# A gated MLP as seven products of halves: its roundings, copies and sums in another queue order, its late weight quarters made earlier, its v in four banks

## The chip, the cores and the metric

One NeuronCore of a Trainium2 chip runs the whole program in one launch. The time is microseconds (us) of device time; of several executions the median is taken. A profile of one more execution gives times from the span's start. The engines are TensorE (PE; PEld is its weight load), VectorE (DVE), ScalarE (ACT), GpSimd (POOL) and SyncE (SP), which issues the DMAs. Each engine works through its own queue in the order in which the code was written; an instruction that waits holds up all that stand behind it.

## The reference, cut to what matters

The input goes through three stages for 4 batches of 768 positions and 384 channels: a gated linear attention, a channel MLP with residual, and a gated MLP that mixes positions:

```python
ch = np.maximum(u @ w_ch1, 0.0) @ w_ch2          # second stage
x = u + ch                                       # (4, 768, 384), goes to x2d in HBM
h = np.maximum(x @ w_in, 0.0)                    # third stage, d_ff = 1024
u, v = h[..., :512], h[..., 512:]
v_n = (v - mean(v)) / np.sqrt(var(v) + 1e-06)    # over the 512 channels
v_s = np.einsum('ts,bsd->btd', w_spatial, v_n) + b_spatial[None, :, None]
out = (u * v_s) @ w_out
```

`w_spatial` is 768 x 768 and comes transposed.

## The kernel before

Matrices are held as two float32r parts, a rounded one (hi, `uh`, `vh`, names that end in h; the rounding is a copy on ScalarE) and the remainder (lo, `ul`, `vl`; `rest`, line 251, a subtraction of the two on VectorE or GpSimd). `mm3` (lines 286 to 288) multiplies two such pairs with three matmuls.

**Stages one and two.** For each batch the channel MLP runs over two blocks of 384 positions with 12 pieces of the inner width each: 24 groups per batch. A group is nine matmuls up (line 379), a ReLU with rounding on ScalarE (`h`, line 386), its remainder on VectorE (`hl`, line 367), and, two groups later, nine matmuls down (`mm3`). The up matmuls use two PSUM banks in turn, so a group can start when the `hl` of the group two before it has been read out of its bank. Between matmuls the code calls `pull()`, six times in a group and 144 times in a batch. With each pull other work is written into the queues, one step of a generator at a time, as many as `due()` allows. Under the first three batches' MLPs that is the attention of the next batch. Under the last batch's, "the last MLP" below, it is the preparation of stage three, `gating_steps`:

- the four quarters of `w_spatial` are loaded (`load_quads`, 576 KB each, in the buffers u0, u1, uh2 and ul2), rounded, combined and split into b11, b21, t3 and t4 (`quad_steps`);
- `w_in` and `w_out` are staged in 12 items through the same four buffers (`Stage`). An item is loaded, its float64 bits are turned to float32 by ScalarE (line 231), VectorE (lines 236 and 239) and an add on GpSimd (line 246); it is rounded by ScalarE (line 277), and VectorE makes the remainder (line 251). A step of the generator begins one item, rounds the one before it and makes the remainder of the one before that;
- the first half of the first batch's x is loaded and split, and three quarters are loaded again for the late parts t1, b22 and t2.

**Stage three**, class `Gating`. `v_n` is cut into 2 x 2 halves, and the product with `w_spatial` is made of seven products of halves (a11 b11, s3 t3, a12 b21, a22 t4, s2 t2, s1 t1, s4 b22) in place of eight. The steps for a batch are:

- `norm`: six tiles of v (`norm_steps`, nine matmuls of 512 columns each into a bank of PSUM), each copied out by ScalarE with ReLU (line 522), statistics on VectorE, then for three tiles together the square root on ScalarE (`z`, line 531), the normalisation (line 540), for the first half a difference (line 545), and for each tile a rounding (`vh`, line 503) and a remainder (`vl`);
- `sums` (lines 557 to 559): three sums per tile on VectorE, then the split of s1;
- `run`: four groups of u into the banks 4 to 7 (`first_half`), the seven products, copies of two of them out of PSUM (`kept`, lines 627 and 630), the split of s4 and s2 (`late_parts`), the gates (lines 589, 594, 596, a remainder on GpSimd), and the projection with `w_out` in two blocks (`project`; its banks are copied out by ScalarE at line 611).

The next batch's `norm` is called before the last projection of a batch and its `sums` after it; this passage from batch to batch is called a seam below. Before the change v goes to the banks 1 and 2 in turn (5 and 6 for the first batch), and the late parts t1, b22 and t2 are made inside the first batch's `norm`, a step between its tiles.

Of the kernel before, what the change touches and what calls it, by code (L numbers as in the profile page):

```python
# [36 lines left out]
F32 = mybir.dt.float32  # L37
# [23 lines left out]
F2 = DFF // 2  # L61
NF2 = F2 // 128
KE = E // 128
TB = 384
# [35 lines left out]
def gla_mixer_gating_kernel(ctx: ExitStack, tc: tile.TileContext, akq, v, vT, u, v3, w12, w_in, wsT, b_sp, w_out, out):  # L100
# [379 lines left out]
    class Gating:  # L480
# [3 lines left out]
        def __init__(self, g, wts, ap, psp, b, rooms=None, banks=(1, 2)):  # L484
# [4 lines left out]
        def norm(self, others=iter(())):  # L489

            a, b = self.norm_steps(0), self.norm_steps(1)
            for steps in (a, a, a, b, a, b, b, b):
                next(steps, None)
                next(others, None)
            drain(others)

        def split(self, names, c, x, engine=nc.gpsimd):

            tag = {"a11": f"{c}", "s4": f"{c}", "a12": f"{c + CB}", "s1": f"s{c}"}[names[0]]
            n = x.shape[1]  # L500
            hi = self.ap.tile([128, n], F32R, name="vh", tag=f"vh{tag}", bufs=1)
            lo = self.ap.tile([128, n], F32R, name="vl", tag=f"vl{tag}", bufs=1)
            nc.scalar.activation(out=hi, in_=x, func=AF.Copy)  # L503
            rest(lo, x, hi, engine)
            for i, name in enumerate(names):
                o = slice(i * F2 // 2, (i + 1) * F2 // 2)
                self.left[name][c] = hi[:, o], lo[:, o]

        def norm_steps(self, half):
# [3 lines left out]
            for j in range(CB):  # L513
                xh, xl = self.x2[half]
                ps = self.psp.tile([128, 512], F32, "ps_v", self.banks[(half * CB + j) % 2])
# [22 lines left out]
            for j in range(CB):  # L538
# [143 lines left out]
    def late_weights(wts, make, pool):  # L682

        tiles = [make(i, F32R) for i in range(5)]
# [5 lines left out]
        last, two = make(5, F32), pool.tile([128, 2 * TB], F32, name="kept", tag="u")  # L690
# [12 lines left out]
    def quad_steps(wts, raws):  # L703

        sp = wts["all"]
        w11, w12q, w22, w21 = raws
# [25 lines left out]
    def late_steps(wts, raws):  # L732
# [7 lines left out]
        combine(w12q, w12q, w11, nc.gpsimd)  # L740
        yield
        lo("b22", w22)
        yield
        hi("t1", w12q)
# [993 lines left out]
```

## Time and profile before

| | us |
|---|---|
| median of three runs (707.42 to 709.40) | 708.81 |
| the profiled execution, device time | 708.43 |
| its span, first to last instruction | 706.6 |
| TensorE busy | 671.7 (95%) |
| VectorE busy | 412.1 (58%) |
| ScalarE busy | 305.9 (43%) |
| GpSimd busy | 186.6 (26%) |
| mean granted TensorE clock, share of full | 0.982 |

The profiled execution's device time stands 1.8 us above its span. The two levels of TensorE's clock are 2.4 GHz (1.00 in the rows) and 1.2 GHz (0.50). The four seams lie at about 452, 522, 587 and 650 us, the last MLP between 355 and 439 us.

### The profile page before, as it was taken

How to read it: one execution, taken by the hardware profiler on the slowest of the kernel's cores; microseconds unless marked ns; L12 is line 12 of the kernel's file. 1: busy time of each engine (PE TensorE's matmuls, PEld its weight loads, DVE VectorE, ACT ScalarE, POOL GpSimd, SP SyncE). 2: the span in 40 equal slices, each digit the busy share in tenths (PEclk: the TensorE clock that was granted, in tenths of full speed). 3: DMA queues.
4: the chain of work that ended last, by engine and by line, in shares of the span. 5: the costliest groups of instructions: out<-in, count | busy, mean ns of one | idle time of the engine just before them, and what ended most of it. 6: DMA issues, size and time to landing. Idle time of an engine off the chain costs nothing.

```text
span 706.6 us, 14545 instructions
## 1 busy us (share of the span) xinstructions
PE 671.7 (95%) x6084; PEld 638.9 (90%) x6084; DVE 412.1 (58%) x762; ACT 305.9 (43%) x599; POOL 186.6 (26%) x169
## 2 busy tenths in 40 slices
PE   7989998999999999999998999799989998998995
PEld 6889987999999999999998999699879987997995
DVE  8989999665455344443336692774473455537441
ACT  3985366755555345454323343532243243233321
POOL 4520001151111301100300245406333440633041
PEclk9999999999999999999999999899989999999998
DMA  9699044444433005001033264202020202100001
GB/s 338 255 325 219 13 78 79 78 94 110 78 69 86 18 8 113 1 2 36 1 104 118 80 198 159 69 1 69 0 65 5 67 1 68 34 34 1 34 33 40
DMA packets 21644, 56.18 MB, mean 80 GB/s; under 512 B 2752, under 2 KB 12864, under 8 KB 20288
## 3 DMA queue, kind: packets, MB, share of 16 engines
q1 hardware_dynamic: 21568, 55.15, 28.5%
q8 instruction: 50, 0.82, 0.5%
q14 instruction: 26, 0.21, 0.1%
HBM read 44.52 MB, written 9.44 MB: 76 GB/s over the span
## 4 chain that ended last, share of the span: by engine, by line
PE 68%; DVE 21%; ACT 5%; issue 2%; DMA 2%; SPq 0%; ACTq 0%; DVEq 0%
PE banks L379 17%; PE banks L286 14%; PE banks L287 14%; PE banks L288 14%; DVE vt L540 2%; PE banks L1035 2%; DVE bw L906 2%; DVE fw L919 2%; DVE hl L367 1%; ACT vh L503 1%; DVE vt L545 1%; DVE narrow L239 1%; PE banks L993 1%; PE banks L1025 1%; PE banks L966 1%
## 5 line engine op out<-in xcount | busy, mean ns | idle before, releaser
L379 PE MATMUL banks<-partuh,w 128*128 128x384 f32 x564 | 131.7, 341 | 4.8 <-DVE hl L367 4.7
L379 PEld LDWEIGHTS banks<-partuh,w 128*128 128x128 f32 x564 | 99.9, 189 | 7.2 <-DVE hl L367 6.0
L367 DVE SCALAR_TENSOR_TENSOR hl<-banks,h 128x384 fp32r<-128x384 f32 x96 | 52.6, 548 | 83.2 <-ACT h L386 82.0
L286 PE MATMUL banks<-h,w 128*128 128x384 f32 x288 | 98.5, 342 | 0.2
L287 PE MATMUL banks<-h,w 128*128 128x384 f32 x288 | 96.7, 336 | 0.0
L288 PE MATMUL banks<-hl,w 128*128 128x384 f32 x288 | 96.5, 335 | 0.0
L386 ACT ACTIVATE h<-banks 128x384 fp32r<-128x384 f32 x94 | 45.5, 485 | 77.1 <-PE banks L379 76.9
L379 PE MATMUL banks<-partul,w 128*128 128x384 f32 x282 | 66.5, 344 | 0.0
L251 POOL TENSOR_TENSOR room<-room 128x384 fp32r<-128x384 f32 x32 | 32.5, 1017 | 112.7 <-ACT room L596 112.4
L895 POOL TENSOR_TENSOR akq<-akq,fw 128x768 f32<-128x768 f32 x14 | 23.6, 1685 | 142.6 <-DVE fw L919 125.3
L251 POOL TENSOR_TENSOR partul<-ub,partuh 128x384 fp32r<-128x384 f32 x43 | 42.6, 1016 | 65.4 <-ACT partuh L322 56.8
L286 PEld LDWEIGHTS banks<-h,w 128*128 128x128 f32 x288 | 54.2, 188 | 1.6 <-issue 0.8
L287 PEld LDWEIGHTS banks<-h,w 128*128 128x128 f32 x288 | 54.3, 188 | 0.0
L288 PEld LDWEIGHTS banks<-hl,w 128*128 128x128 f32 x288 | 54.2, 188 | 0.0
L379 PEld LDWEIGHTS banks<-partul,w 128*128 128x128 f32 x282 | 49.7, 190 | 0.8
L286 PE MATMUL banks<-partuh,winh 128*128 128x384 f32 x96 | 35.5, 370 | 14.4 <-ACT room L611 9.7
L503 ACT ACTIVATE vh<-vt 128x512 fp32r<-128x512 f32 (+1 forms) x48 | 26.4, 577 | 45.4 <-DVE vt L545 18.3
L596 ACT ACTIVATE room<-room 128x384 fp32r<-128x384 f32 x32 | 16.8, 525 | 67.3 <-DVE room L594 67.3
L251 DVE TENSOR_TENSOR vl<-vt,vh 128x512 fp32r<-128x512 f32 (+1 forms) x32 | 20.8, 672 | 29.5 <-ACT vh L503 28.0
L287 PE MATMUL banks<-partuh,winl 128*128 128x384 f32 x96 | 34.8, 362 | 0.0
L288 PE MATMUL banks<-partul,winh 128*128 128x384 f32 x96 | 34.6, 361 | 0.0
L895 POOL TENSOR_TENSOR akq<-akq,bw 128x768 f32<-128x768 f32 x11 | 18.6, 1691 | 60.3 <-DVE bw L906 49.8
(252 smaller groups left out, 1525.0 us busy)
## 6 DMA issues: line engine op xcount, KB each, us to landing
akq<-in_akq SPq DMA_DIRECT2D x24, 434.4 KB, 7.2
bits<-in_w SPq DMA_DIRECT2D x12, 768.0 KB, 11.6
x2d<-ub SPq DMA_DIRECT2D x8, 576.0 KB, 4.2
ub<-x2d SPq DMA_DIRECT2D x8, 576.0 KB, 4.3
out_y<-room SPq DMA_DIRECT2D x24, 192.0 KB, 2.0
v<-in_v SPq DMA_DIRECT2D x15, 288.0 KB, 8.1
words<-in_wsT SPq DMA_DIRECT2D x7, 576.0 KB, 5.0
words<-in_w_in SPq DMA_DIRECT2D x8, 384.0 KB, 3.6
```

Source lines behind the costliest of these rows:

```text
L251: engine.tensor_tensor(out=out, in0=x, in1=hi.bitcast(F32), op=ALU.subtract)
L286: nc.tensor.matmul(out=ps, lhsT=wh, rhs=xh, start=first, stop=False, skip_group_check=more)
L287: nc.tensor.matmul(out=ps, lhsT=wl, rhs=xh, start=False, stop=False, skip_group_check=more)
L288: nc.tensor.matmul(out=ps, lhsT=wh, rhs=xl, start=False, stop=last, skip_group_check=more)
L367: nc.vector.scalar_tensor_tensor(out=hl, in0=ps[:, 0:TB], scalar=0.0, in1=h.bitcast(F32), op0=ALU.max, op1=ALU.subtract)
L379: nc.tensor.matmul(out=ps[:, 0:TB], lhsT=wx[:, k * 128 : (k + 1) * 128], rhs=ux[:, k, :], start=i == 0, stop=i == len(parts) - 1)
L386: nc.scalar.activation(out=h, in_=ps[:, 0:TB], func=AF.Relu)
L503: nc.scalar.activation(out=hi, in_=x, func=AF.Copy)
L540: nc.vector.tensor_scalar(out=vt, in0=vt, scalar1=st[:, j, 0:1], scalar2=r[:, j : j + 1], op0=ALU.subtract, op1=ALU.mult)
L596: nc.scalar.activation(out=hi, in_=x, func=AF.Copy)
L895: engine.tensor_tensor(out=chunks(x)[:, c], in0=chunks(x)[:, c], in1=chunks(by)[:, c, 1:CW], op=ALU.mult)
L906: nc.vector.tensor_tensor_scan(out=bw[:, ::-1], data0=a[:, 1 : AW + 1][:, ::-1], data1=ends[:, ::-1], initial=0.0, op0=ALU.mult, op1=ALU.max)
```

## The change

- `split` becomes `splits`: for three tiles first all the roundings, then all the remainders, all of these on VectorE (before, four of the six remainders of a batch were GpSimd's).
- In `norm` the order is a, a, a, b, a, b, a, b, b: the splits of the first half come a step later, those of the second half are held back (`rest_of_norm`) until `sums`, which stands behind the projection. The split of s1 goes from `sums` to `late_parts`.
- v goes to the banks 1, 2, 4, 5, 1, 2 (first batch: 5, 6, 7, 5, 6, 7).
- `late_steps` runs in the last MLP's tail, from the 116th pull on, with its two combinations on VectorE instead of GpSimd; it no longer stands between the first batch's tiles of v.
- The generator of the last MLP takes a step at every third pull (before: 31 steps in 129 pulls, one in 4.16). The loads of the quarters stay at the 13th pull; their first use moves from the 21st to the 25th. The quarter that is needed second now is loaded second.

```diff
-        def __init__(self, g, wts, ap, psp, b, rooms=None, banks=(1, 2)):
+        def __init__(self, g, wts, ap, psp, b, rooms=None, banks=(1, 2, 4, 5, 1, 2)):
...
-        def norm(self, others=iter(())):
+        def norm(self):
             a, b = self.norm_steps(0), self.norm_steps(1)
-            for steps in (a, a, a, b, a, b, b, b):
+            for steps in (a, a, a, b, a, b, a, b, b):
                 next(steps, None)
-                next(others, None)
-            drain(others)
+            self.rest_of_norm = b
...
+        def splits(self, pieces):
+            made = []
+            for names, c, x in pieces:
...
+                nc.scalar.activation(out=hi, in_=x, func=AF.Copy)
+                made.append((lo, x, hi))
...
+            for lo, x, hi in made:
+                rest(lo, x, hi, nc.vector)
...
-                ps = self.psp.tile([128, 512], F32, "ps_v", self.banks[(half * CB + j) % 2])
+                ps = self.psp.tile([128, 512], F32, "ps_v", self.banks[half * CB + j])
...
-                    self.split(("a11", "s3"), j, vt)
-                else:
-                    self.split(("a12", "a22"), j, vt, nc.vector if j else nc.gpsimd)
+            yield
+            self.splits([(("a12", "a22") if half else ("a11", "s3"), j, self.vt[half * CB + j]) for j in range(CB)])
         def sums(self):
+            drain(self.rest_of_norm)
...
-            self.split(("s1",), c, a11, nc.vector)
         def late_parts(self):
-            for c in range(CB):
-                self.split(("s4", "s2"), c, self.vt[c + CB], nc.vector)
+            self.splits([(("s4", "s2"), c, self.vt[c + CB]) for c in range(CB)])
+            self.splits([(("s1",), c, self.vt[c][:, 0 : F2 // 2]) for c in range(CB)])
...
         def gating_steps():
             yield from check_alpha()
+            while pulls < 13:
+                yield
+            raws = load_quads(up.pool, RAW, (0, 3, 1, 2))
             yield
             yield
-            raws = load_quads(up.pool, RAW, range(4))
...
-            late_raws.extend(load_quads(up.pool, RAW[1:], range(3)))
+            raws = load_quads(up.pool, RAW[1:], range(3))
...
-            yield
+            while pulls < 116:
+                yield
+            late_weights(wts, late_tile)
+            yield from late_steps(wts, raws)
...
         def due():
+            if b == B - 1:
+                return -(-pulls // 3)
...
-        cur = Gating(g, wts, gpool, ps, 0, banks=(5, 6))
+        cur = Gating(g, wts, gpool, ps, 0, banks=(5, 6, 7, 5, 6, 7))
...
-        cur.norm(late_steps(wts, late_raws))
+        cur.norm()
```

TensorE's order stays the same but for one small matmul of the input check. Three places in the other queues follow; the line numbers of the change are its own.

ScalarE at a seam, before. `vt` is a v tile coming out of PSUM, `z` the square root, `vh` the rounding of a tile, `room<-banks` the copy of the projection out of its banks, `late<-banks` the copies of two products.

```order
L522 ACTIVATE vt<-banks 128x512 x4
L531 ACTIVATE z<-xe 128x3
L503 ACTIVATE vh<-vt 128x512 x3
L522 ACTIVATE vt<-banks 128x512 x2
L531 ACTIVATE z<-xe 128x3
L503 ACTIVATE vh<-vt 128x512 x3
L611 ACTIVATE room<-banks 128x384 x3
L503 ACTIVATE vh<-vt 128x256 x3
L627 ACTIVATE late<-banks 128x384 x2
L630 ACTIVATE late<-banks 128x384 x2
```

The same place of the change:

```order
L525 ACTIVATE vt<-banks 128x512 x4
L534 ACTIVATE z<-xe 128x3
L525 ACTIVATE vt<-banks 128x512
L504 ACTIVATE vh<-vt 128x512 x3
L525 ACTIVATE vt<-banks 128x512
L534 ACTIVATE z<-xe 128x3
L614 ACTIVATE room<-banks 128x384 x3
L504 ACTIVATE vh<-vt 128x512 x3
L630 ACTIVATE late<-banks 128x384 x2
L633 ACTIVATE late<-banks 128x384 x2
L504 ACTIVATE vh<-vt 128x512 x3
L504 ACTIVATE vh<-vt 128x256 x3
```

The three copies of the projection now stand ahead of the second half's roundings, and the roundings of s1 (128x256) behind the copies of the products.

VectorE in the last MLP, before, while `w_in` is staged. L236 and L239 belong to the item that is begun, L251 is the remainder of the one two before it, `hl` the remainder that a group of the MLP needs.

```order
L367 SCALAR_TENSOR_TENSOR hl<-banks,h 128x384
L251 TENSOR_TENSOR winl<-words,winh 128x384
L236 TENSOR_SCALAR words<-words 128x384
L239 SCALAR_TENSOR_TENSOR words<-words 128x384
L367 SCALAR_TENSOR_TENSOR hl<-banks,h 128x384
L251 TENSOR_TENSOR winl<-words,winh 128x384
L236 TENSOR_SCALAR words<-words 128x384
L239 SCALAR_TENSOR_TENSOR words<-words 128x384
L251 TENSOR_TENSOR winl<-words,winh 128x384
```

The same place of the change:

```order
L367 SCALAR_TENSOR_TENSOR hl<-banks,h 128x384
L251 TENSOR_TENSOR winl<-words,winh 128x384
L236 TENSOR_SCALAR words<-words 128x384
L239 SCALAR_TENSOR_TENSOR words<-words 128x384
L251 TENSOR_TENSOR winl<-words,winh 128x384
L236 TENSOR_SCALAR words<-words 128x384
L239 SCALAR_TENSOR_TENSOR words<-words 128x384
L367 SCALAR_TENSOR_TENSOR hl<-banks,h 128x384
```

Two items now stand between one group's `hl` and the next, where one or two stood before.

VectorE at the end of the last MLP, before. `ub` are the sums that end the MLP, `s` and `mv` the statistics of v tiles, `late` the remainders of the late parts.

```order
L367 SCALAR_TENSOR_TENSOR hl<-banks,h 128x384 x4
L439 TENSOR_TENSOR ub<-banks,ub 128x384 x3
L524 BN_STATS s_5018<-vt 128x6
L525 BN_AGGR mv<-s_5018 128x2
L524 BN_STATS s_5034<-vt 128x6
L525 BN_AGGR mv<-s_5034 128x2
L251 TENSOR_TENSOR late<-words,late 128x1152
L524 BN_STATS s_5049<-vt 128x6
```

The same place of the change:

```order
L367 SCALAR_TENSOR_TENSOR hl<-banks,h 128x384 x3
L706 TENSOR_TENSOR words<-words 128x1152
L367 SCALAR_TENSOR_TENSOR hl<-banks,h 128x384
L251 TENSOR_TENSOR late<-words,late 128x1152
L706 TENSOR_TENSOR words<-words 128x1152
L367 SCALAR_TENSOR_TENSOR hl<-banks,h 128x384
L251 TENSOR_TENSOR late<-words,late 128x1152
L251 TENSOR_TENSOR late<-words,late 128x384 x3
L367 SCALAR_TENSOR_TENSOR hl<-banks,h 128x384 x3
L439 TENSOR_TENSOR ub<-banks,ub 128x384 x3
L527 BN_STATS s_5028<-vt 128x6
```

The late parts, combinations (L706) and remainders, went from among the v tiles into the MLP's last groups.

## Rows read from the trace of the kernel before

**Rows 1.** The page's groups: xcount | busy, mean ns | idle before, releaser.

```profile
L367 DVE SCALAR_TENSOR_TENSOR hl<-banks,h 128x384 fp32r<-128x384 f32 x96 | 52.6, 548 | 83.2 <-ACT h L386 82.0
```

**Rows 2.** Timeline of TensorE, four waits: start, us, what, [idle before <-releaser].

```profile
376.94 0.92 PE L379 MATMUL banks<-partuh,w 128*128 128x384 f32 x2 [2.61 <-DVE hl L367]
...
457.32 0.69 PE L286 MATMUL banks<-partuh,winh 128*128 128x384 f32 x1 [4.70 <-ACT vt L522]
...
471.81 0.44 PE L286 MATMUL banks<-wspb21h,vh 128*128 128x384 f32 x1 [0.86 <-ACT late L627]
...
525.14 0.69 PE L286 MATMUL banks<-partuh,winh 128*128 128x384 f32 x1 [3.25 <-ACT room L611]
```

**Rows 3.** Stretches after waits: length, busy by engine, PEclk, DMA share, GB/s.

```profile
376.90:380.50 3.60, 3.56 (x11) 3.56 (x12) 3.57 (x4) 0.92 (x1) 0.00 (x0) 0.53 0.00 0
457.30:462.40 5.10, 5.08 (x16) 5.08 (x17) 4.59 (x15) 0.73 (x3) 0.00 (x0) 0.50 0.00 0
525.10:530.70 5.60, 5.56 (x17) 5.56 (x18) 4.90 (x13) 2.01 (x5) 0.00 (x0) 0.50 0.66 211
590.30:596.00 5.70, 5.65 (x32) 5.65 (x33) 4.91 (x13) 2.50 (x6) 0.00 (x0) 1.00 0.68 211
653.40:656.90 3.50, 3.48 (x11) 3.48 (x12) 3.14 (x9) 1.56 (x4) 0.00 (x0) 0.52 0.47 169
```

**Rows 4.** Timeline of ScalarE at the seam after 518 us.

```profile
519.25 0.20 ACT L531 ACTIVATE z<-xe 128x3 f32<-128x3 f32 x1 [1.49 <-DVE xe L530]
...
521.07 1.15 ACT L503 ACTIVATE vh<-vt 128x512 fp32r<-128x512 f32 x2 [1.62 <-DVE vt L540]
...
524.62 1.23 ACT L611 ACTIVATE room<-banks 128x384 f32<-128x384 f32 x3
```

**Rows 5.** Timeline of VectorE at the same seam.

```profile
511.34 0.55 DVE L540 TENSOR_SCALAR vt<-vt,mv,r 128x512 f32<-128x512 f32 x1
...
513.18 1.52 DVE L540 TENSOR_SCALAR vt<-vt,mv,r 128x512 f32<-128x512 f32 x1
...
524.74 0.69 DVE L251 TENSOR_TENSOR vl<-vt,vh 128x512 fp32r<-128x512 f32 x1 [0.69 <-ACT vh L503]
...
526.72 0.42 DVE L251 TENSOR_TENSOR vl<-vt,vh 128x256 fp32r<-128x256 f32 x1
```

**Rows 6.** Timeline of GpSimd at the same seam.

```profile
513.09 2.75 POOL L251 TENSOR_TENSOR vl<-vt,vh 128x512 fp32r<-128x512 f32 x2 [7.03 <-ACT vh L503]
```

**Rows 7.** The chain that ended last, in the last MLP: start, us, what.

```profile
388.13 1.56 PE banks L379 x9
...
416.61 1.86 PE banks L379 x9
```

**Rows 8.** Timeline of ScalarE, last MLP, first roundings of the quarters.

```profile
374.75 1.16 ACT L707 ACTIVATE wspb21h<-words 128x1152 fp32r<-128x1152 f32 x1 [4.63 <-DMA words<-in_wsT]
```

**Rows 9.** Tile words, 360 to 392 us: ns min/median/max, first and last start.

```profile
L701 DVE TENSOR_TENSOR words<-words x4: 1347/1350/1359, 376.8 to 384.7; 128x1152 f32<-128x1152 f32 x4
```

**Rows 10.** The page's DMA issues: KB each, median us from issue to landing.

```profile
words<-in_w_in SPq DMA_DIRECT2D x8, 384.0 KB, 3.6
```

**Rows 11.** Timeline of GpSimd, adds of the weight staging, last MLP.

```profile
402.98 1.02 POOL L246 TENSOR_TENSOR words<-words 128x384 uint32<-128x384 uint32 x1 [1.08 <-ACT words L231]
...
406.82 1.12 POOL L246 TENSOR_TENSOR words<-words 128x384 uint32<-128x384 uint32 x1 [2.82 <-DVE words L239]
...
411.62 1.03 POOL L246 TENSOR_TENSOR words<-words 128x384 uint32<-128x384 uint32 x1 [1.51 <-ACT h L386]
...
414.16 1.12 POOL L246 TENSOR_TENSOR words<-words 128x384 uint32<-128x384 uint32 x1 [1.51 <-ACT h L386]
...
416.41 1.02 POOL L246 TENSOR_TENSOR words<-words 128x384 uint32<-128x384 uint32 x1 [1.13 <-ACT words L231]
```

**Rows 12.** Timeline of TensorE and GpSimd, second batch's first projection.

```profile
549.61 0.34 PE L286 MATMUL banks<-wouth,room 128*128 128x384 f32 x1
...
549.81 2.07 POOL L251 TENSOR_TENSOR room<-room 128x384 fp32r<-128x384 f32 x2 [0.84 <-ACT room L596]
```

More of the change, by code (lines that the diff above doesn't have):

```diff
@@ L680, in thirds, with late_weights @@
         return [t[:, i * TB : (i + 1) * TB] for i in range(CB)]
-    def late_weights(wts, make, pool):
-        tiles = [make(i, F32R) for i in range(5)]
+    def late_weights(wts, make):
+        tiles = [make(i) for i in range(5)]
         for i, x in enumerate(LATE[0:2]):
@@ L689, in late_weights, with kept_rooms @@
         wts["sp"][LATE[2]] = [free[0:CB], free[CB : 2 * CB]]
-        last, two = make(5, F32), pool.tile([128, 2 * TB], F32, name="kept", tag="u")
+    def kept_rooms(last, pool):
+        two = pool.tile([128, 2 * TB], F32, name="kept", tag="u")
         return [*thirds(last), last[:, QUAD : QUAD + TB], two[:, 0:TB], two[:, TB : 2 * TB]]
@@ L705, in quad_steps @@
         sp = wts["all"]
-        w11, w12q, w22, w21 = raws
+        w11, w21, w12q, w22 = raws
         hi = lambda n, x: nc.scalar.activation(out=sp[n][0], in_=x, func=AF.Copy)
@@ L739, in late_steps @@
         hi("b22", w22)
-        combine(w12q, w12q, w11, nc.gpsimd)
+        combine(w12q, w12q, w11, nc.vector)
         yield
+        hi("t1", w12q)
         lo("b22", w22)
         yield
-        hi("t1", w12q)
-        combine(w11, w22, w12q, nc.gpsimd)
+        combine(w11, w22, w12q, nc.vector)
         yield
-        yield
-        lo("t1", w12q)
         for x, h, _ in t2:
             nc.scalar.activation(out=h, in_=x, func=AF.Copy)
-        yield
+        lo("t1", w12q)
         yield
@@ L1497, in gating_steps, with late_tile @@
             x2_first.append(load_x2(0, 1, up))
-            yield
+            while pulls < 116:
+                yield
+            late_weights(wts, late_tile)
+            yield from late_steps(wts, raws)
         pulls, done = 0, 0
-        x2_first, late_raws = [], []
+        x2_first = []
+        def late_tile(i, ty=F32R):
+            return wp0.tile([128, QUAD + TB], ty, name="late", tag=f"f{i}")
         def pull():
@@ L1541, in gla_mixer_gating_kernel @@
                 gating = Stage(gp, gating_items(wts), [(up.pool, x, KE * TB) for x in RAW])
-                steps, n_steps = gating_steps(), len(gating.items) + 19
+                steps = gating_steps()
             pulls, done = 0, 0
@@ L1560, in gla_mixer_gating_kernel @@
         spatial_bias(g, cp)
-        kept = late_weights(wts, lambda i, ty: wp0.tile([128, QUAD + TB], ty, name="late", tag=f"f{i}"), cp)
-        cur = Gating(g, wts, gpool, ps, 0, banks=(5, 6))
+        cur = Gating(g, wts, gpool, ps, 0, banks=(5, 6, 7, 5, 6, 7))
         cur.x2 = [x2_first[0], split_x2(x2_first[1], up, 1)]
-        cur.norm(late_steps(wts, late_raws))
+        cur.norm()
         cur.sums()
-        cur.rooms = GatingRooms(up.pool, kept)
+        cur.rooms = GatingRooms(up.pool, kept_rooms(late_tile(5, F32), cp))
         for b in range(B):
@@ L1658, in gla_mixer_gating_kernel @@
                 wts2 = gating_weights(gw2)
-                kept2 = late_weights(wts2, lambda i, ty: gw2.tile([128, QUAD + TB], ty, name=f"late{i}"), cp2)
-                drain(quad_steps(wts2, load_quads(up2.pool, RAW, range(4))))
+                late_tile2 = lambda i, ty=F32R: gw2.tile([128, QUAD + TB], ty, name=f"late{i}")
+                late_weights(wts2, late_tile2)
+                kept2 = kept_rooms(late_tile2(5, F32), cp2)
+                drain(quad_steps(wts2, load_quads(up2.pool, RAW, (0, 3, 1, 2))))
                 drain(late_steps(wts2, load_quads(up2.pool, RAW[1:], range(3))))
```

17 lines of the change are left out of this document (7 added, 10 removed).

## The prediction

> **What bounds the kernel now.** I read the page's busy times first (the table above), then its groups of instructions, then TensorE's timeline for its idle stretches, then the queue of the engine that ended each. TensorE is busy 95% of the span, so the time can fall only where it waits or runs at half clock. From the last MLP on, the timeline has six waits of 0.8 us or more; four stand in [rows 2], and the third and fourth seam repeat the 3.25 us of its last row. Three facts are to be seen in them.
>
> The wait before 376.94 us, 2.61 us, is released by VectorE's `hl` (0.55 us each, and itself mostly waiting for `h` [rows 1]), but the root is in ScalarE's queue: there the rounding of the second quarter waited 4.63 us for a DMA and ran only at 374.75 [rows 8], with two groups' `h` behind it. That quarter was the last of four to be loaded.
>
> The waits of 4.70 and 3.25 us end with a copy out of PSUM on ScalarE. TensorE needs a bank whose contents have long been complete, and the copy stands behind three roundings. At 521.07 two roundings run, the third after VectorE has normalised its tile, and only at 524.62 the three copies of the projection [rows 4]. The wait of 0.86 us is the same with the copies of two products.
>
> After four of the five waits of over 2.5 us the granted clock was at the lower level. TensorE then ran busy for 3.56, 5.08, 5.56 and 3.48 us at 0.50 to 0.53; after the third seam it stayed at 1.00 [rows 3].
>
> **What the change takes away at the seams.** TensorE's order is kept, so I ask for each wait whether its releaser comes early enough. In the new ScalarE queue the three copies of the projection need only `z` ahead of them. With `z` as late as now, 519.25 + 0.20 [rows 4], a first copy of 0.5 us ends at about 520, and TensorE needs its bank at 525.14 - 3.25 = 521.9 [rows 2]: 1.9 us to spare. Does `z` come later? On VectorE three remainders of 0.69 us [rows 5] now stand ahead of the last statistics, 2.1 us. In return GpSimd no longer makes two remainders there (2.75 us for two [rows 6]), during which a normalisation took 1.52 instead of 0.55 us [rows 5] and the difference behind it grew alike: about 1.9 us back. So `z` moves by about 0.2, and all three 3.25 us go.
>
> At the first seam the last v tile's copy still stands behind three roundings, but its bank is needed only by the fourth group of u, not the second, and the late parts are gone from between. I estimate 1.6 us to spare there and take 4.70 as gone. The 0.86 us goes because the roundings of s1 now stand behind the copies of the products. The moved remainders of the second half run under the four groups of u and two products, ten of TensorE's microseconds; if that cover failed, the products would wait as the copies do now.
>
> Waits: 4.70 + 0.86 + 3 x 3.25 = 15.3 us. With them go the half-clock stretches at three seams: 5.08/2 + 5.56/2 + 3.48 x 0.48 = 7.0 us [rows 3]. Together -22.3 us.
>
> **What the change does in the last MLP.** First the quarters. The second one used is now the second loaded, and one group's `h` stands between the two roundings, so the 2.61 us wait and 3.56 x 0.47 = 1.7 us of half clock behind it [rows 3] go: 4.3 us. VectorE then has six operations of 1.35 us [rows 9] between the landing of the last quarter (374.75, [rows 8]) and the end of t4's remainder, with three `hl` of 0.55 between, and one rounding of 1.16 that it waits for. That gives 374.75 + 8.1 + 1.7 + 1.2 = 385.8, less half a microsecond that overlaps: 385.3. Each `hl` falls 0.3 to 0.8 us before its group would start, so nothing waits yet.
>
> Then the items. The second item's buffer is free at 385.3; its load takes 3.6 us [rows 10], and from there to the add I take 1.3 us, which is GpSimd's idle time between two adds, where VectorE makes the same steps (1.1 to 1.5 [rows 11]). Its add on GpSimd starts at about 390.2. How fast can items follow? The adds of now come every 2.54 us where a group's `hl` stands between (411.62 to 414.16) and 2.25 us where none does (414.16 to 416.41); with the three closing sums of a block between it was 3.84 (402.98 to 406.82) [rows 11]. The cycle is VectorE's: the remainder is held up while GpSimd's add runs, then the next item's two steps follow, then the next add. Nothing in the change shortens it. With one `hl` to two items it is 2.4 us, and the block's three sums add 1.4. But the generator now asks for an item every third pull, half a group, and a group is 3.12 us long (416.61 - 388.13 is 9 groups and 0.4 us [rows 7]): an item every 1.56 us. Now it asks at every 4.16th pull, 2.16 us, and the queues fall behind only slowly.
>
> So from the second item on VectorE sets TensorE's pace, since a group's `hl` stands behind two items and the group after next cannot start without it. The eleventh item's add starts at 390.2 + 9 x 2.4 + 1.4 = 413.2. The `hl` of the 15th group stands just before it, so the 17th group starts at 413.6. The `hl` of the 16th stands behind another item and a remainder: about 417.0, where the 18th starts; the 19th starts at 420.1. Now it starts at 416.61 [rows 7]: +3.5 us, the 4.3 us saved before included. Before the 17th group TensorE waits 3.1 us, as long as at the seams, two of which in three were followed by half clock. I take 3.4 us of it, 1.7 us lost, 1.5 after the 18th group's wait has covered a little. Last MLP: +5.0 us.
>
> The late parts cost nothing in the tail. They are four operations of 1.35 us [rows 9] and three of a third of the size, 7 us of VectorE, in four groups of 3.12 us where `hl` takes 0.55 each. If that cover were gone, the first tiles of v would start up to 2 us later. Their loads are issued as the last items free their buffers, some 7 us ahead of the first use. TensorE's order is otherwise unchanged, and no part before the last MLP moves.
>
> **The sum.** Span 706.6 - 22.3 + 5.0 = 689.3 us. The profiled execution stood 1.8 above its span, at 708.43, which is 0.4 below the median of the runs shown: **691.1 us**.
>
> **A rule of the skill beside the row.** A normalisation that met GpSimd's remainders took 1.52 instead of 0.55 us [rows 5, 6], and the adds' interval is short only where a remainder ran ahead of the add [rows 11]. The Trainium skill, "SBUF — State Buffer", section "Who interferes with whom", says that a VectorE instruction with two SBUF inputs and a GpSimd instruction that reads SBUF exclude each other, the second waiting for the whole of the first. The rows agree as far as they go. By the rule taken strictly no remainder would run beside an add and every item would take the longer interval, 2.54 us: the sum would be 9 x 0.14 = 1.3 higher, 692.4. By the rows it is 691.1.
>
> **Rivals.**
>
> - *The pace does not hold TensorE.* If the slack between `h` and `hl` swallows the items, the last MLP loses its 4.3 us and the 0.4 at the 19th group and gains nothing: 706.6 - 22.3 - 4.7 + 1.8 = 681.4. For it: now the adds fall behind their pulls too, at 0.3 us an item, and TensorE lost just 0.4. Against it: eleven items fall behind by 0.8 each, 9 us, and two banks give about 3. 0.14.
> - *Every remainder is held up*, 2.54 us an item as worked out above, or an item takes still longer while TensorE's clock is low: 692.4 to 695. Nothing forbids it, since the two kinds of interval mix by chance. 0.16.
> - *The later gates starve the projection.* Three remainders of 0.42 us [rows 5] now stand ahead of the first gates, 1.3 us. GpSimd's remainder for the third quarter of the projection ends at 549.81 + 1.03 = 550.8 (half of two); the projection begins at 549.61 [rows 12], its third quarter 18 matmuls of 0.175 us later, 552.8. 1.9 us of slack become 0.7. From 1.9 us of delay on TensorE would wait; at 1.5 us in each of four batches: 697. 0.10.
> - *The change does not do what it says*: `z` comes 2 us later than now, so the copies are still late and a wait of 1 to 3 us with its half clock stays at the seams: 698 to 706. Against it the balance of 2.1 and 1.9 above. 0.04.
> - *Slower than before.* The pace eats the seams' 22.3 us. For that the last MLP would have to lose 17.3 us more than forecast, and an item take 17.3/9 = 1.9 more than 2.4: 4.3 us. The longest interval now is 3.84, with three extra sums in it [rows 11]. 0.02.
>
> **Numbers.** The forecast as worked out, 688 to 692.4, has 0.54. Its unknowns are the item's cycle (2.25 to 2.54 us: -1.4 to +1.3), the half clock (0 or 1.5) and the start of the items (1 us either way). Its own range with the second rival is 687 to 695. The range 684 to 698 takes in both, the third rival and a part of the first: about 0.82. A measurement of this kernel can tell 0.3% (2.1 us) from no change. Faster 0.96, same 0.02, slower 0.02.
>
> **What would show it.** Right: no TensorE idle over 0.5 us at the four seams and a clock of 1.00 there; ScalarE's copies of the projection within 1 us of the end of its matmuls; no wait before the 7th group of the last MLP; then adds on GpSimd every 2.2 to 2.6 us, with TensorE waiting 1 to 3 us for `hl` before each of the 13th to 18th group, and the 24th group starting about 4 to 5 us later than now. Wrong: items at 1.6 us without such waits (681), or waits at the first projection or at the first gates of the batches (697), or a seam whose copies come behind `z` at 521 or later.

## The result, and the profile after

The changed kernel takes **689.19 us** (median of 4 runs, 688.84 to 690.38); the kernel before took 708.12 beside it (706.89 to 709.4). The ratio is 0.9736, 95% interval 0.9713 to 0.9759. The forecast was 691.1. The profiled execution took 689.03 us, its span is 687.1 (706.6 before). Its page begins:

```profile
PE 664.9 (97%) x6084; PEld 633.3 (92%) x6084; DVE 411.3 (60%) x780; ACT 305.8 (45%) x599; POOL 159.6 (23%) x151
```

The span falls by 19.5 us. The first tile of v starts at 441.92 us (438.59 before), so the part before it got 3.3 us longer and the rest, from there to the end, went from 268.0 to 245.2 us: 22.8 shorter. The sum of TensorE's waits from 355 us on (engine and line that waits, releaser: us, times, longest) holds nothing of a seam any more:

```profile
PE banks L286 <- DVE ub L439: 3.5, 1, 3.5
PE banks L379 <- DVE hl L367: 2.5, 2, 1.4
```

All three are in the last MLP. Of before [rows 2], the 2.61, 4.70, 0.86 and the three 3.25 are gone. Stretches of the changed kernel, with the columns of [rows 3] (length, busy time of PE, PEld, DVE, ACT and POOL, PEclk, DMA share, GB/s):

```profile
407.40:411.20 3.80, 3.72 (x13) 3.75 (x14) 3.73 (x8) 1.59 (x4) 1.45 (x2) 0.55 0.57 190
454.00:471.00 17.00, 17.00 (x98) 16.96 (x97) 16.06 (x41) 8.58 (x18) 0.00 (x0) 1.00 0.00 1
514.00:531.00 17.00, 17.00 (x99) 17.00 (x98) 10.09 (x23) 6.61 (x14) 0.00 (x0) 1.00 0.22 69
```

At these two seams TensorE is busy without a break at full clock, and so it is at the other two (573 to 590 and 633 to 650 us). Up to its last matmul half clock is left once, after the longest wait of the last MLP.

The seam on ScalarE, which answers to [rows 4]:

```profile
512.98 0.20 ACT L534 ACTIVATE z<-xe 128x3 f32<-128x3 f32 x1 [2.50 <-DVE xe L533]
513.09 1.41 ACT L614 ACTIVATE room<-banks 128x384 f32<-128x384 f32 x3
514.80 1.67 ACT L504 ACTIVATE vh<-vt 128x512 fp32r<-128x512 f32 x3 [0.30 <-DVE vt L543]
```

The copies of the projection (L614, L611 before) run right behind `z`, the three roundings behind them. The same seam on VectorE, which answers to [rows 5]:

```profile
508.32 0.54 DVE L543 TENSOR_SCALAR vt<-vt,mv,r 128x512 f32<-128x512 f32 x1
508.89 0.42 DVE L548 TENSOR_TENSOR vt<-vt 128x256 f32<-128x256 f32 x1
509.23 0.69 DVE L527 BATCH_NORM_STATS2 s<-vt 128x6 f32<-128x512 f32 x1
...
510.05 1.86 DVE L251 TENSOR_TENSOR vl<-vt,vh 128x512 fp32r<-128x512 f32 x3
511.83 0.69 DVE L527 BATCH_NORM_STATS2 s<-vt 128x6 f32<-128x512 f32 x1
...
512.77 0.17 DVE L533 TENSOR_SCALAR xe<-mv 128x3 f32<-128x3 f32 x1
```

No row here has idle time ahead of it. The third normalisation takes 0.54 us (1.52 before), the fifth tile's statistics stand ahead of the three remainders, and VectorE goes straight on to `xe`.

The adds of the items on GpSimd, which answer to [rows 11]:

```profile
390.01 1.22 POOL L246 TENSOR_TENSOR words<-words 128x384 uint32<-128x384 uint32 x1 [2.13 <-ACT h L386]
...
406.72 1.01 POOL L246 TENSOR_TENSOR words<-words 128x384 uint32<-128x384 uint32 x1 [1.14 <-ACT words L231]
409.82 1.11 POOL L246 TENSOR_TENSOR words<-words 128x384 uint32<-128x384 uint32 x1 [2.09 <-DVE words L239]
412.07 1.02 POOL L246 TENSOR_TENSOR words<-words 128x384 uint32<-128x384 uint32 x1 [1.14 <-ACT words L231]
```

Eight adds lie from 390.01 to 406.72, 2.39 us each; with the closing sums of the first block between two of them the interval is 3.10. And VectorE in the same stretch, from one `hl` past the next:

```profile
396.77 0.55 DVE L367 SCALAR_TENSOR_TENSOR hl<-banks,h 128x384 fp32r<-128x384 f32 x1
397.24 1.37 DVE L251 TENSOR_TENSOR winl<-words,winh 128x384 fp32r<-128x384 f32 x1
398.53 0.35 DVE L236 TENSOR_SCALAR words<-words 128x384 uint32<-128x384 uint32 x1
...
399.39 0.55 DVE L251 TENSOR_TENSOR winl<-words,winh 128x384 fp32r<-128x384 f32 x1
399.86 1.19 DVE L236 TENSOR_SCALAR words<-words 128x384 uint32<-128x384 uint32 x1
...
401.56 0.55 DVE L367 SCALAR_TENSOR_TENSOR hl<-banks,h 128x384 fp32r<-128x384 f32 x1
...
406.31 0.55 DVE L367 SCALAR_TENSOR_TENSOR hl<-banks,h 128x384 fp32r<-128x384 f32 x1
406.78 1.48 DVE L439 TENSOR_TENSOR ub<-banks,ub 128x384 f32<-128x384 f32 x3
```

Two whole items (L251, L236 and, left out here, L239 of each) stand between two `hl`, and the engine never idles: 4.79 us for what TensorE does in 3.12. In each item one instruction that runs beside GpSimd's add is long (1.37 instead of 0.55, 1.19 instead of 0.35). TensorE pays for it here (its timeline, as in [rows 2]):

```profile
397.38 0.79 PE L379 MATMUL banks<-partuh,w 128*128 128x384 f32 x3 [1.09 <-DVE hl L367]
...
402.16 0.79 PE L379 MATMUL banks<-partuh,w 128*128 128x384 f32 x3 [1.39 <-DVE hl L367]
...
407.48 0.41 PE L286 MATMUL banks<-h,w 128*128 128x384 f32 x1 [3.48 <-DVE ub L439]
```

The last is the first matmul down of the second block. It needs an accumulator bank which the closing sums (L439) free, and these stand behind two items and an `hl`. From 407.48 to 450 us TensorE has no wait of 0.4 us or more.

### The profile page after: what moved, and what is told of

Its sections match the earlier page's. It is cut to its first block, busy times and chain, and to the rows that moved or that the text cites. A ratio compares the mean times of both kernels' runs of the same rounds, so it can differ in the third digit from the quotient of the medians.

```text
span 687.1 us, 14557 instructions
## 1 busy us (share of the span) xinstructions
PE 664.9 (97%) x6084; PEld 633.3 (92%) x6084; DVE 411.3 (60%) x780; ACT 305.8 (45%) x599; POOL 159.6 (23%) x151
## 4 chain that ended last, share of the span: by engine, by line
PE 76%; DVE 15%; ACT 3%; DMA 3%; issue 2%; SPq 0%; DVEq 0%; ACTq 0%
PE banks L286 17%; PE banks L288 17%; PE banks L287 17%; PE banks L379 16%; PE banks L1038 2%; DVE bw L909 2%; DVE fw L922 2%; PE banks L996 1%; DVE hl L367 1%; PE banks L1028 1%; DVE narrow L239 1%; PE banks L969 1%; DVE narrow L246 1%; PE banks L953 1%; DVE w L251 1%
## 5 line engine op out<-in xcount | busy, mean ns | idle before, releaser
L251 POOL TENSOR_TENSOR room<-room 128x384 fp32r<-128x384 f32 x32 | 32.5, 1016 | 168.4 <-ACT room L599 168.2
L251 POOL TENSOR_TENSOR partul<-ub,partuh 128x384 fp32r<-128x384 f32 x43 | 42.6, 1017 | 76.5 <-ACT partuh L322 56.8
L251 DVE TENSOR_TENSOR vl<-vt,vh 128x512 fp32r<-128x512 f32 (+1 forms) x48 | 26.6, 616 | 20.4 <-ACT vh L504 20.4
L288 PE MATMUL banks<-partul,winh 128*128 128x384 f32 x96 | 32.1, 334 | 0.0
L288 PE MATMUL banks<-woutl,room 128*128 128x384 f32 x96 | 32.1, 334 | 0.0
L286 PE MATMUL banks<-wouth,room 128*128 128x384 f32 x96 | 32.1, 334 | 0.0
L287 PE MATMUL banks<-wouth,room 128*128 128x384 f32 x96 | 32.1, 334 | 0.0
```

Source lines behind the costliest of these rows:

```text
L251: engine.tensor_tensor(out=out, in0=x, in1=hi.bitcast(F32), op=ALU.subtract)
L286: nc.tensor.matmul(out=ps, lhsT=wh, rhs=xh, start=first, stop=False, skip_group_check=more)
L287: nc.tensor.matmul(out=ps, lhsT=wl, rhs=xh, start=False, stop=False, skip_group_check=more)
L288: nc.tensor.matmul(out=ps, lhsT=wh, rhs=xl, start=False, stop=last, skip_group_check=more)
```

## The experiments

Times are medians beside runs of the kernel before on the same chip, in brackets the ratio's 95% interval. The changed kernel stands at 0.9736 (0.9713 to 0.9759).

**1. The kernel before, remainders behind all three normalisations.** GpSimd keeps its remainders, the banks and the place of the copies stay.

```diff
                     nc.vector.tensor_tensor(out=y, in0=x, in1=y, op=ALU.subtract)
+            for j in range(CB):
+                vt = self.vt[half * CB + j]
+                if half == 0:
                     self.split(("a11", "s3"), j, vt)
```

> The kernel before with one edit: in each half the three tiles are normalised first, then rounded, then their remainders made (before: tile by tile). Engines, banks, late parts, pace, and the place of the projection's copies behind the roundings all stay. The prediction's theory (the copies are late because they stand behind the roundings): the wait of 3.25 us stays at the three later seams to within 1 us; 706 to 709 us. The rival (the roundings were late only because VectorE made a remainder, held up by GpSimd's, ahead of the third normalisation): by the trace of before, z comes about 1.9 us earlier and the third rounding another 1.5 us, the waits fall below 0.5 us and the half clock goes with them: 708.1 - 9.8 - 4.4 = 694 us, within 2.

699.17 us, 0.9863 (0.9831 to 0.9895): between the two. TensorE's waits:

```profile
PE banks L286 <- ACT vt L522: 4.7, 1, 4.7
PE banks L286 <- ACT room L614: 3.8, 3, 1.3
```

Each 3.25 became 1.28, without half clock behind it. ScalarE shows why it is not zero:

```profile
519.62 0.20 ACT L531 ACTIVATE z<-xe 128x3 f32<-128x3 f32 x1 [1.49 <-DVE xe L530]
521.44 1.67 ACT L503 ACTIVATE vh<-vt 128x512 fp32r<-128x512 f32 x3 [1.62 <-DVE vt L540]
523.01 1.24 ACT L614 ACTIVATE room<-banks 128x384 f32<-128x384 f32 x3
```

The third rounding no longer waits for a normalisation that stands behind a remainder, but the copies still stand behind all three.

**2. The kernel before, copies of the projection first.** Only the second half's split moves behind the copies.

```diff
                 next(others, None)
             drain(others)
+            self.rest_of_norm = b
...
-                    self.split(("a12", "a22"), j, vt, nc.vector if j else nc.gpsimd)
+                    continue
+            if half:
+                yield
+                for j in range(CB):
+                    self.split(("a12", "a22"), j, self.vt[CB + j], nc.vector if j else nc.gpsimd)

         def sums(self):
+            drain(self.rest_of_norm)
```

> The kernel before with one thing altered: the roundings and remainders of the second half of v stand behind the copies of the projection. Engines, banks, and the order in the first half stay as before. Theory A, of the prediction: the three waits of 3.25 us were the place of the copies in ScalarE's queue, behind three roundings. All three go, with two stretches of half clock; the first seam keeps its 4.70, and the time is 694 to 697. Theory B, from the run in which the remainders stood behind the normalisations: of each 3.25 us some 2 is the remainder ahead of the third normalisation and 1.28 the place of the copies. In this kernel both go as well, because the remainder now stands behind both; but z itself is as late as before, so at most 0.3 us of wait is left and the time is 694 to 698. What would speak against both: waits of over 1 us at these three seams, and over 700 us.

694.48 us, 0.9812 (0.9789 to 0.9834), as both theories had it. The waits that are left:

```profile
PE banks L286 <- ACT vt L523: 4.7, 1, 4.7
PE banks L379 <- DVE hl L367: 3.3, 2, 3.0
```

All three waits of 3.25 us are gone, though `z` comes no earlier than before and GpSimd keeps its remainders. The 0.86 went too.

**3. The changed kernel, copies behind the roundings again.**

```diff
-            for steps in (a, a, a, b, a, b, a, b, b):
+            for steps in (a, a, a, b, a, b, a, b, b, b):
```

> The changed kernel with the split of the second half put back ahead of the projection's copies in ScalarE's queue; remainders on VectorE, four banks, pace and late parts stay. The prediction's theory: the copies are late again, 3.25 us and its half clock at three seams: 700 to 703 us. The rival: in the changed kernel's trace the third rounding ends at 516.47 and TensorE needs the bank at about 516.9, so the copies come 0 to 0.5 us late: 689 to 691 us.

690.67 us, 0.9747 (0.9715 to 0.9778), not told apart from the changed kernel, and no seam waits, as the rival had it.

```profile
512.74 0.20 ACT L534 ACTIVATE z<-xe 128x3 f32<-128x3 f32 x1 [2.51 <-DVE xe L533]
514.56 1.68 ACT L504 ACTIVATE vh<-vt 128x512 fp32r<-128x512 f32 x3 [1.62 <-DVE vt L543]
516.14 1.23 ACT L614 ACTIVATE room<-banks 128x384 f32<-128x384 f32 x3
```

**4. The changed kernel, four of the six remainders on GpSimd as before.**

```diff
+                engine = nc.gpsimd if names[0] == "a11" or (names[0] == "a12" and c == 0) else nc.vector
-                rest(lo, x, hi, nc.vector)
+                rest(lo, x, hi, engine)
```

> The changed kernel with four of six remainders of a batch back on GpSimd (all of the first half, the first of the second). Both theories of order: no wait comes back, since the roundings no longer alternate with normalisations; 688.5 to 690.5 us, z some 0.5 us earlier or later. The rival, that VectorE's time free of GpSimd is what matters: z comes 2 us later and a part of the waits returns, 692 to 700 us.

689.59 us, 0.9731 (0.9699 to 0.9762): no difference. One wait of 0.40 us is new at the first seam (ScalarE's copy of the sixth tile, then TensorE):

```profile
458.61 0.58 ACT L526 ACTIVATE vt<-banks 128x512 f32<-128x512 f32 x1
459.24 0.44 PE L286 MATMUL banks<-partuh,winh 128*128 128x384 f32 x1 [0.40 <-ACT vt L526]
```

The four runs and the two kernels agree in one table. It counts from the first matmul of the projection (512.35 us before, 507.49 after) at the second seam:

| kernel | `z` | copies begin | TensorE waits |
|---|---|---|---|
| before | 6.90 | 12.27 | 3.25 |
| 1, remainders behind the normalisations | 6.91 | 10.31 | 1.28 |
| 2, copies first | 6.91 | 7.02 | 0 |
| 3, changed, copies behind | 5.49 | 8.90 | 0 |
| 4, changed, GpSimd | 6.12 | 6.23 | 0 |
| changed | 5.49 | 5.60 | 0 |

From the first two rows, 1.96 us earlier is 1.97 less wait, so the copies must begin by 12.27 - 3.25 = 9.02. Number 3 makes that by 0.12. The remainder ahead of the third normalisation was worth 1.96, a `z` earlier by 1.41 the rest of number 3, and the copies' place alone 5.25. Either the last suffices or the first two together, these by the 0.12 only.

**5. The changed kernel, v in two banks.**

```diff
-        def __init__(self, g, wts, ap, psp, b, rooms=None, banks=(1, 2, 4, 5, 1, 2)):
+        def __init__(self, g, wts, ap, psp, b, rooms=None, banks=(1, 2, 1, 2, 1, 2)):
...
-        cur = Gating(g, wts, gpool, ps, 0, banks=(5, 6, 7, 5, 6, 7))
+        cur = Gating(g, wts, gpool, ps, 0, banks=(5, 6, 5, 6, 5, 6))
```

> The changed kernel with v in two banks again (1 and 2 in turn, 5 and 6 for the first batch). Expected by the trace: nothing at the later seams; at the first seam the last tile's copy ended at 457.47 and the third group of u, which would need its bank, begins at 457.3, so 0.2 to 0.5 us: 689 to 690.5 us. The rival, that four banks are what keeps v running: a wait of 1 to 3 us at each seam, 693 to 700 us.

690.43 us, 0.9743 (0.9712 to 0.9775), as the trace had it: no wait is listed at a seam, and the third group of u at the first one begins 0.2 us late. Alone, the banks carry nothing that can be measured.

**6. The changed kernel, late parts back in the first `norm`.**

```diff
+                next(others, None)
+            drain(others)
...
-            while pulls < 116:
-                yield
-            late_weights(wts, late_tile)
-            yield from late_steps(wts, raws)
+            late_raws.extend(raws)
+            yield
...
-        cur.norm()
+        late_weights(wts, late_tile)
+        cur.norm(late_steps(wts, late_raws))
```

> The changed kernel with the late parts put back among the six tiles of v of the first batch, as before, with their sums on VectorE as in the changed kernel. Theory A, the late parts between the tiles were one of the things that delayed the copies at the first seam: a wait of 2 to 4.7 us comes back there, with half clock behind it, and the time is 692 to 696. Theory B, four banks and the roundings gathered at the end cover them, and the tail of the last MLP gets lighter: no wait over 0.5 us at the first seam, and 688 to 690.

690.72 us, 0.976 (0.9737 to 0.9784): the second theory as to the first seam, where no wait came back. The 0.8 us of new waits lie further on, at the first gates, and the time is 0.7 us above that theory's range.

**7. Numbers 5 and 6 together.**

```diff
-        def __init__(self, g, wts, ap, psp, b, rooms=None, banks=(1, 2, 4, 5, 1, 2)):
+        def __init__(self, g, wts, ap, psp, b, rooms=None, banks=(1, 2, 1, 2, 1, 2)):
...
+        cur.norm(late_steps(wts, late_raws))
```

> The changed kernel with two of its parts undone together, which undone singly brought no wait over 0.6 us at the first seam: the late parts are back among the first batch's tiles of v, and v goes to two banks. Theory A, the 4.70 us at the first seam fell in portions: the new order puts the copy of the fifth tile ahead of the roundings, the late parts cost 1.4 us (with them the last tile's copy ended at 458.8, without them at 457.4), and the banks decide whether that copy is needed by the third group of u (at about 457.4) or the fourth. Then both undone give a wait of 1.2 to 1.6 us before the third group of u, less than 4.70, and 690.5 to 692.5. Theory B, either the late parts or the banks alone carried the 4.70: undone together a wait of 3 us or more comes back with its half clock, and 694 to 697.

691.4 us, 0.9759 (0.9726 to 0.9793). ScalarE and TensorE at the first seam:

```profile
455.32 0.58 ACT L527 ACTIVATE vt<-banks 128x512 f32<-128x512 f32 x1
457.49 0.63 ACT L506 ACTIVATE vh<-vt 128x512 fp32r<-128x512 f32 x1 [1.59 <-DVE vt L550]
...
459.86 0.58 ACT L527 ACTIVATE vt<-banks 128x512 f32<-128x512 f32 x1
```

TensorE waits 1.60 us (458.89 to 460.49) for the last row, the sixth tile's copy, and keeps its full clock. So the first theory holds: late parts and banks were worth about 1.6 of the 4.70, each covering for the other. What is left of the 4.70 is 3.1 us by subtraction. A part of it fits the copy of the fifth tile, which now runs ahead of the roundings (455.32); in the kernel before it came behind them, at 456.69, and the second group of u waited for its bank. Another part is the remainders: number 4 undoes only these, and the sixth tile's copy then begins 16.92 us after the first matmul of v (441.69), in the changed kernel 14.97 (456.89 and 441.92). Four banks leave 0.40 of that as a wait. No run divides the 3.1 between the two, and the fifth copy's place was not undone by itself.

**8. The changed kernel, items asked for less often.** From the 56th pull of the last MLP one at every fourth pull instead of every third.

```diff
-                return -(-pulls // 3)
+                if pulls <= 55:
+                    return -(-pulls // 3)
+                if pulls <= 111:
+                    return 19 - (-(pulls - 55) // 4)
+                return 33 - (-(pulls - 111) // 3)
...
-            while pulls < 116:
+            while pulls < 124:
```

> The changed kernel with one thing altered: from the 56th pull of the last MLP on an item is asked for at every fourth pull instead of every third, in the last part at every third again, and the late parts begin at the 124th pull. Theory A, the pace lets items pile up ahead of the groups' remainders and closing sums on VectorE: the waits of 1.09, 1.39 and 3.48 us before the 14th, 15th and 16th group shrink, the 24th group starts at 429 to 432 instead of 435.68 us, and the time is 4 to 6 us below that of the changed kernel, 683 to 685. Theory B, VectorE's work in these groups is the same in sum and is only placed elsewhere: the waits move to the later groups or to the first tiles of v, the 24th group starts within 1 us of 435.7 and the time stays at 688 to 691.

684.43 us, 0.9662 (0.9642 to 0.9682): the first theory. Waits of 1.59 and 0.81 us are left in the last MLP, the clock stays at 1.00 and v starts at 436.85. The last item's add starts at 414.69, with the faster pace at 414.61: asking later loses VectorE nothing.

**9. The changed kernel, adds on VectorE.**

```diff
-            x = both_parts(words, t, nc.vector if self.begun in self.adders else nc.gpsimd) if wide else words
+            x = both_parts(words, t, nc.vector if self.begun in self.adders or self.alone else nc.gpsimd) if wide else words
...
                 steps = gating_steps()
+                gating.alone = True
```

> The changed kernel with one thing altered: the adds that join an item's two halves run on VectorE instead of GpSimd in the last MLP. Theory A, an item's 2.4 us comes from VectorE and GpSimd holding each other up: without GpSimd an item takes 2.0 to 2.2 us on VectorE, the 24th group starts 1 to 2 us earlier and the time is 687 to 688.5. Theory B, VectorE was working through most of the 2.4 us and now has one more operation of about 0.7 us for each item: an item takes 2.6 to 3.1 us, the 24th group starts 2 to 6 us later and the time is 691 to 695.

688.77 us, 0.9735 (0.9711 to 0.976): neither. TensorE's three waits in the last MLP are 1.13, 1.10 and 3.25 us, in the changed kernel 1.09, 1.39 and 3.48, and v starts 0.24 us earlier, at 441.68. VectorE over the same two items:

```profile
397.06 0.55 DVE L367 SCALAR_TENSOR_TENSOR hl<-banks,h 128x384 fp32r<-128x384 f32 x1
397.52 0.55 DVE L251 TENSOR_TENSOR winl<-words,winh 128x384 fp32r<-128x384 f32 x1
397.99 0.35 DVE L236 TENSOR_SCALAR words<-words 128x384 uint32<-128x384 uint32 x1
...
399.07 0.56 DVE L246 CUSTOM_DVE_ANT_0 words<-words 128x768 uint16<-128x768 uint16 x1
...
401.58 0.55 DVE L367 SCALAR_TENSOR_TENSOR hl<-banks,h 128x384 fp32r<-128x384 f32 x1
```

No instruction is long any more, but each item has an add of 0.56 us more: 4.52 us from `hl` to `hl` instead of 4.79. An item takes 2.25 us. GpSimd had held VectorE up for about 0.8 us of an item's 2.39; the rest is VectorE's own work, to which the add now belongs, and `hl` still stands behind two items.

**10. Numbers 8 and 9 together.**

```diff
+                    return 19 - (-(pulls - 55) // 4)
...
+                gating.alone = True
```

> The slower pace of the run before, and the items' adds on VectorE as well. With the adds there an item took 2.25 instead of 2.39 us, and the two waits that the slower pace left in the last MLP were 1.59 and 0.81 us. Theory A, VectorE's time per item is still what these two waits come from: they shrink to 0.5 to 1.2 us together, and the time is 683 to 684.2. Theory B, the 1.59 is the closing sums behind a group's own remainder, whatever the items take: it stays, and the time is 684 to 685.

685.1 us, 0.967 (0.9645 to 0.9695). The 1.59 became 1.19 and the 0.81 four waits of 0.25 to 0.50: 2.8 us in sum, not less than 2.4. v started at 437.92, no earlier than without the adds; the time is the second theory's, give or take 0.1.

**11. An item at every 4.5th pull.** As number 8, with these lines:

```diff
+                if pulls <= 118:
+                    return 19 - (-(pulls - 55) * 2 // 9)
+                return 33 - (-(pulls - 118) // 3)
```

> The changed kernel with an item asked for at every 4.5th pull (2.34 us, about the 2.39 that an item takes) from the 56th pull on. Theory A, the waits come from items asked for faster than VectorE makes them: none of over 1 us is left in the last MLP, and the time is 682.5 to 684. Theory B, the items that now lie later push the late parts and the last MLP's tail: a wait of 1 to 3 us moves to the last groups or the first tiles of v, and the time is 684.5 to 687.

682.69 us, 0.9633 (0.9607 to 0.966): the first theory. The last MLP, columns as above:

```profile
355.00:435.40 80.40, 80.29 (x463) 79.68 (x462) 57.05 (x89) 33.29 (x64) 18.70 (x18) 1.00 0.45 140
```

There is no wait left, and v starts at 435.42. From there to the end of the span (680.8) it is 245.4 us, with the changed kernel 245.2. The gain in the last MLP is greater than the starts of v show, since in this execution it begins 1.5 us later than in the changed kernel (its first group at 356.69, there at 355.22), behind a stretch of half clock at 122 us that the last section shows. From that first group to v it is 78.73 us, in the changed kernel 86.70, in number 8 81.68, in the kernel before 83.50. VectorE has now mostly one item between two `hl`:

```profile
395.41 0.55 DVE L367 SCALAR_TENSOR_TENSOR hl<-banks,h 128x384 fp32r<-128x384 f32 x1
...
398.21 0.56 DVE L367 SCALAR_TENSOR_TENSOR hl<-banks,h 128x384 fp32r<-128x384 f32 x1
...
400.74 0.56 DVE L367 SCALAR_TENSOR_TENSOR hl<-banks,h 128x384 fp32r<-128x384 f32 x1
401.22 1.48 DVE L439 TENSOR_TENSOR ub<-banks,ub 128x384 f32<-128x384 f32 x3
```

**12. Numbers 11 and 9 together.**

```diff
+                    return 19 - (-(pulls - 55) * 2 // 9)
...
+                gating.alone = True
```

> The pace of 4.5 pulls with the items' adds on VectorE (2.25 us an item, asked for every 2.34). Theory A: no wait of over 0.5 us in the last MLP, and the time is 682 to 683.5. Theory B, as for the pace of 4.5 alone: 684.5 to 687.

683.46 us, 0.9641 (0.9614 to 0.9667): a wait of 0.41 us is left, as the first theory had it, and nothing is gained over number 11. Numbers 8 and 11 are shown faster than the changed kernel; which of them is the faster the intervals leave open.

## Why the prediction was right, step by step

**The seams, -22.3 forecast, -22.8 measured** from the first tile of v to the end. All waits and all half clock behind them went, as forecast. The stated cause, the copies' place behind three roundings, was put to the test by number 2, which changed nothing else and took away all three waits of 3.25 us and two half-clock stretches. But it isn't the only way: number 3 undoes that part in the changed kernel and no wait comes back. The prediction saw one cause where the change brings two, each of them enough. For the 0.86 its reason, the roundings of s1 behind the copies of the products, isn't needed either: in number 2 they still stand ahead of these copies, and the wait went.

**`z`, forecast 0.2 us later, came 1.4 earlier** (5.49 after the projection's first matmul, 6.90 before). The balance of 2.1 for three remainders and 1.9 back was nearly right (1.78 to the sixth tile's statistics, and 1.9 for the long normalisation and difference). It left out VectorE's idle time. In the kernel before, the fifth tile's copy stood behind the third rounding on ScalarE, and VectorE waited 1.19 us for it before the statistics of two tiles; number 1 has the same wait, 1.18. In the changed kernel the remainders fill it. 1.78 - 1.95 (the two long rows, less 0.54 and 0.42) - 1.19 gives -1.36. In number 4, where GpSimd makes remainders again, `z` stands at 6.12, between the two.

**The first seam.** 1.6 us to spare were forecast; the sixth tile's copy ended at 457.47, its bank was needed at about 458.9: 1.4. Its reasons were the banks and the late parts. Number 7 shows that these two were worth 1.6 of 4.70. The bank for which the second group of u waited before was the fifth tile's (its copy began at 456.69, the group at 457.32), not the last one's, and what freed that one, the new order and the remainders, the prediction doesn't name for this seam. That the whole 4.70 went was forecast on a part of its causes, and to that extent it was luck.

**The last MLP, +5.0 forecast, +3.3 measured**: the mis-sized term. The quarters came out as forecast, no wait before the 7th group. The items' cycle, 2.4 forecast, is 2.39. What was too long is the chain behind it. The closing sums cost 0.7, not 1.4, and the eleventh add started at 412.07, not 413.2. The `hl` of the 15th and 16th group ended at 412.22 and 415.31, where 413.6 and 417.0 were forecast: 1.4 and 1.7 too late. The half clock came as forecast (1.7 us, in 3.72 us at 0.55), and it wasn't covered. The 17th and 18th group started at 413.84 and 416.96, each 1.6 us behind the `hl` it needs. So without the half clock the start of the 18th would have been about 415.4. With the two errors against each other the 18th group's start, 417.0 before the clock's term, was hit by luck. The longest wait was forecast for `hl` ahead of the 17th group; it came ahead of the first matmul down of the second block, for the closing sums, which the prediction had in VectorE's queue but didn't follow to the banks that they free. Waits for `hl` before each of the 13th to 18th group were among its signs; only the 14th and 15th had one (1.09 and 1.39).

**The rivals.** *The pace does not hold TensorE* was priced at 681.4. It didn't come true, but numbers 8 and 11 show that the pace was the cause and the price nearly right. It had the last MLP 4.7 us shorter than before; number 11 has it 4.8 shorter (78.73 against 83.50), and runs at 682.69. *Every remainder is held up*: the rows go further, since in each item one instruction was held, the remainder or L236, by 0.8 us, and still an item took 2.39, not 2.54. The longer interval only meant that a group's `hl` stood in it. The rule of the Trainium skill ("SBUF — State Buffer", "Who interferes with whom"), on VectorE instructions with two inputs in SBUF, agrees for the remainder, which has two and took 1.37 us instead of 0.55. L236 here (1.19 instead of 0.35) and the normalisation that the prediction puts beside that rule (1.52 instead of 0.55) have one such input tile, so that sentence of it doesn't cover them. *The later gates*: the projection of the next batch began at 539.07, GpSimd's remainder for its third quarter ended at 541.06 and was needed at 542.2, so 1.1 us were to spare, 0.7 forecast.

## What to carry to other kernels

Ask for each wait not only what stands ahead of its releaser, but what that engine itself was waiting for: a queue's idle time is where added work is free, and it was missing from the one balance that came out with the wrong sign. When work is fed into another loop by a pace, compare the interval asked for with the interval that the slowest engine needs: here 1.56 against 2.39 us cost TensorE 8.0 us (86.70 us from the last MLP's first group to v, 78.73 in number 11), and the last add came only 0.3 us sooner after that group (59.39 against 59.71). Two parts of a change that each suffice look useless when undone one at a time, so undo them together, or do each alone on the kernel before.

## What the runs showed of the hardware

A wait of TensorE doesn't always bring half clock. Waits of 1.28 us (number 1) and 1.60 us (number 7) left it at 1.00; after the 3.48 us in the changed kernel it fell. Ahead of 122 us all these kernels run the same code, and TensorE has one wait of 1.1 to 2.2 us there. In the kernel before, after 2.10 us, the clock stayed at 1.00; in number 11, after 1.82 us, it fell (the same stretch of before, and then of number 11):

```profile
122.10:125.50 3.40, 3.40 (x104) 3.10 (x103) 0.52 (x2) 3.35 (x7) 0.00 (x0) 1.00 0.02 5
```

```profile
122.10:125.50 3.40, 3.40 (x59) 3.05 (x57) 0.54 (x2) 3.32 (x6) 0.00 (x0) 0.50 0.00 0
```

Of the fourteen executions profiled here it fell there in three, after 1.82, 1.94 and 2.15 us, and stayed at 1.00 in eleven, after 1.15 to 2.12. So in this range it differs from one execution to the next. In number 11 the last MLP began 1.5 us later for it. That some of the spread between runs comes from it is argued, not shown.
